# Another order of issue in the attention phase of a delta-rule attention and two gated feed-forward layers

## The chip, the cores and the metric

The kernel runs on one core of a Trainium2 chip. The metric is device time in microseconds (us), the median of several runs. The core has five engines with a queue each, worked off in order: TensorE (PE, matmuls), VectorE (DVE), ScalarE (ACT), GpSimd (POOL) and SyncE (SP, which only issues transfers here). An engine whose next instruction must wait stands still, whatever lies behind it.

## The reference

Three layers follow each other, in float32, with the weights given in float64.

```python
def _attn_ref(q, k, v, beta):                     # B, H, S, D = 4, 8, 768, 48
    k_n = k / (np.linalg.norm(k, axis=-1, keepdims=True) + 1e-06)
    state = np.zeros((B, H, D, D))
    for t in range(S):
        y[:, :, t] = einsum('bhd,bhde->bhe', q[:, :, t], state)
        v_old = einsum('bhde,bhd->bhe', state, k_n[:, :, t])
        state = state + beta_t * einsum('bhd,bhe->bhde', k_n[:, :, t], v[:, :, t] - v_old)
def _moe_ref(x, w_gate, w_val, w_out, rms_g):     # 3072 tokens, 384 -> 1536 -> 384
    xn = x / np.sqrt(np.mean(x * x, axis=-1, keepdims=True) + 1e-06) * rms_g
    g = xn @ w_gate
    return (g * sigmoid(g) * (xn @ w_val)) @ w_out
def _moe2_ref(x, w_in, w_out):                    # 384 -> 2048 -> 384
    h = x @ w_in
    return (h * tanh(softplus(h))) @ w_out
```

## The kernel before

The sequence of 768 steps is cut into 12 rows of 64 steps, for all 32 heads at once. Within a row the recurrence becomes matrix products with the inverse of a triangular 64x64 matrix per head; from row to row the state `sx` is carried. Two rows form a segment `sg`, and `rl` is a row's place in it. Everything is done in pairs of a high and a low half (`xh`, `xl`), three matmuls for one product.

The program has three phases. `phase_b1` (lines 343 to 1228) holds the attention of all rows and, beside it, the first layer's gated units of two of its six pairs of 256 columns (`part_a`, made by `gated`). `phase_b2` does the other four pairs, and `phase_c` the last layer. Weights come as 64-bit numbers and are converted on the chip, half a block at a time (`prepare_half`, `convs`): a load, a magnitude on ACT (L168; on DVE L170 where `act` is false), four bit steps on DVE (L172, L175, L180, L183), a high part on ACT (L194; or DVE) and a low part on DVE or GpSimd (L197).

The order in which instructions are issued is written by the program itself. Each strand of work is a generator that issues a piece and yields a weight. `plan` (L44) runs the strands of the start, rows 0 and 1: each has a list of times in `P`, and the strand whose next time is the lowest goes next (a time that lies before the strand's last one means: at once). `merge` (L62) runs the strands of each later row: it takes the strand with the smallest share of its total done. The numbers are arbitrary units; only the order that they give reaches the chip, and each engine works through its own part of that order.

The strands that the change and the prediction speak of:

- `quick_lane(sg)` (L761): the inverse of 16x16 blocks for rows 0 to 3, on DVE: the diagonal (ACT L626, DVE L627), transposes (L779), the scaled matrix Nw (L789 to L793), steps i2 to i7 (L802, L806), and then for each row `rl` two T8 steps (L818, L822) and two transposes (L830 to L841).
- `quick_products(r)` (L847), five calls, here a to e: a is a PE product and Zq on DVE (L863); b a product and the copy of X11 on ACT (L875); c a product, copies and the first half of `merge32` (L739); d a product and copies (L886); e the second half of `merge32` (L749, L753), after which row r's values can be computed.
- `inlane(sg)`, driven by `lanes`: the inverse for rows 4 to 11, nearly all on DVE (L627 to L719).
- `chain_row(r)`: the stages of a row, in an order given by a list of names: r residual (PE L940, DVE L945), nA and nB the norm and scaling of the keys of row r+4 (DVE L537, POOL L550, L561), q0 and q1 transposes of q (PE L620, ACT L621), y the product with the state (L958), p the scores (PE L600, DVE mask L610), v the values (PE L983, ACT L988), k the state update (PE L1032, DVE L1037), o0 and o1 the outputs (PE L999, ACT L1007, L1013), s0 and s1 their scaling (ACT L1044), x0 and x1 the input of the first layer (PE L1057, ACT L1060, then `xl`), c0 and c1 transposes of the keys of row r+4, g their products. S, T, X, Y are s0, s1, x0, x1 of the row before.
- `part_a`: gated steps of nine matmuls each (L259 to L261), with Silu on ACT (L311), and products back (L293 to L295). `DUE` says how many units of it go beside each row.

PSUM has five banks for all of the attention's products (`bank`), two for the gated units.

Of the kernel before, what the change touches and what calls it, by code (L numbers as in the profile page):

```python
# [20 lines left out]
    XB=2, WE=16, RB=4, TB=4, LANE=18.8, AFTER=6.2, LD=3.0, CVT=9.0, CVB0=0, CVB1=64.0, PSD=1, NU=4, LAG=4, XD=9, PD=12, SQ=5,  # L21
    ROW="r nA q0 q1 S p T nB y X v Y k c0 o0 c1 o1 g".split(),
    R0="r q0 q1 p v k o0 o1 s0 s1 x0 x1 c0 c1 g".split(),
    R1="r nA q0 q1 y p nB v k o0 o1 s0 s1 x0 c0 c1 g".split(),
    R2="r nA Y q0 q1 p nB y v k c0 o0 c1 o1 g".split(),
    RL="r q0 q1 S p T y X Y v o0 k o1".split(),
    DUE=[0, 6, 5, 11],
    CVS=[0, 0, 6.5, 0],
    C=dict(n=0.2, q=0.5, r=1.4, y=1.1, p=1.2, v=1.2, o=0.9, k=1.2, s=0.1, x=0.45, c=0.4, d=0.4, g=1.2, h=1.2),

    ROW0=[24.0, 24.1, 24.4, 46.4, 46.6, 48.6, 49.5, 50.0, 51.0, 51.5, 52.0, 54.0, 62.0, 62.5, 90.0],
    ROW1=[52.5, 54.5, 55.0, 55.5, 56.0, 57.0, 60.0, 60.5, 62.5, 63.5, 64.0, 65.0, 65.5, 66.0, 84.0, 84.5, 90.5],
# [66 lines left out]
def kernel(  # L99
# [17 lines left out]
    C = 64  # L117
# [225 lines left out]
    def phase_b1():  # L343
# [417 lines left out]
        def quick_lane(sg):  # L761
# [14 lines left out]
            offs = [t[:, 544:1056].rearrange("p (u c) -> p u c", c=32) for t in (N_, X_)]  # L776
            for rl in range(2):
# [31 lines left out]
            for rl in range(2):  # L809
                r = 2 * sg + rl  # L810
                Nv, Xv = Nw[:, rl], Xw[:, rl]
                for x, y, d in (
# [30 lines left out]
                )  # L843
                halves[r] = [t.rearrange("p (u c) -> p u c", c=32) for t in (Yd, YT)] + [offs[rl]]
                yield 1.75

        def quick_products(r):  # L847
# [17 lines left out]
            )  # L865
            yield 2.8
# [21 lines left out]
            yield from m32  # L888
# [9 lines left out]

# [15 lines left out]
        def chain_row(r):  # L914
# [8 lines left out]
            def turn_q(bp):  # L923
                turn(qp, bp, QT, ("Q", r, bp))
# [123 lines left out]
            def to_x(bp):  # L1048
# [12 lines left out]
                if r >= P["XD"]:  # L1061
# [48 lines left out]
        def order(r):  # L1110
            return P[f"R{r}"] if r < 3 else P["RL"] if r >= NR - 2 else P["ROW"]

# [3 lines left out]
        def finish_a(r):  # L1116
            par = tp.tile([128, KD, T], F32, tag="par", name="par", bufs=1)
# [273 lines left out]
```

## Time and profile before

| | |
|---|---|
| median of 3 runs | 1177.6 us (1176.66 to 1181.1) |
| profiled execution, its own time | 1181.6 us |
| span, first to last instruction | 1179.9 us, 33143 instructions |
| mean granted TensorE clock | 0.949 |
| PE, weight loads (PEld) | 1112.7 us (94%), 1083.1 us (92%) |
| DVE | 615.0 us (52%) |
| ACT | 387.3 us (33%) |
| POOL | 408.4 us (35%) |

The busy times are sums over the whole span, and the three phases have different limits, so the table says little about the attention phase, which takes some 440 us of it; the rows below go by stretch. A granted clock of 1.0 is 2.4 GHz, of 0.5 it is 1.2 GHz; in between is a mean over both.

### The profile page before, as it was taken

How to read it: one execution, taken by the hardware profiler on the slowest of the kernel's cores; microseconds unless marked ns; L12 is line 12 of the kernel's file. 1: busy time of each engine (PE TensorE's matmuls, PEld its weight loads, DVE VectorE, ACT ScalarE, POOL GpSimd, SP SyncE). 2: the span in 40 equal slices, each digit the busy share in tenths (PEclk: the TensorE clock that was granted, in tenths of full speed). 3: DMA queues.
4: the chain of work that ended last, by engine and by line, in shares of the span. 5: the costliest groups of instructions: out<-in, count | busy, mean ns of one | idle time of the engine just before them, and what ended most of it. 6: DMA issues, size and time to landing. Idle time of an engine off the chain costs nothing.

```text
span 1179.9 us, 33143 instructions
## 1 busy us (share of the span) xinstructions
PE 1112.7 (94%) x14712; PEld 1083.1 (92%) x14712; DVE 615.0 (52%) x1039; ACT 387.3 (33%) x822; POOL 408.4 (35%) x364
## 2 busy tenths in 40 slices
PE   5678779999999889999999999999999999999998
PEld 5677678989898889999999999999999999999998
DVE  6656798898987988777676732221111111111111
ACT  4365735676656663222222210111111111111110
POOL 2021035455432442444444432243333333333331
PEclk8656788999999999999999999999999999999999
DMA  9031323333324554443446432611110101111101
GB/s 165 3 70 42 111 56 83 83 90 80 80 83 132 155 203 159 127 142 122 130 139 204 159 122 81 228 54 41 41 41 31 27 25 41 41 41 41 41 1 27
DMA packets 130847, 104.48 MB, mean 89 GB/s; under 512 B 81008, under 2 KB 113264, under 8 KB 130704
## 3 DMA queue, kind: packets, MB, share of 16 engines
q1 hardware_dynamic: 118608, 78.77, 24.0%
q10 hardware_dynamic: 12096, 23.60, 6.1%
q8 instruction: 115, 1.88, 0.7%
q14 instruction: 28, 0.23, 0.1%
HBM read 69.31 MB, written 33.03 MB: 87 GB/s over the span
## 4 chain that ended last, share of the span: by engine, by line
PE 79%; DVE 14%; ACT 2%; SPq 2%; issue 2%; POOL 1%; DMA 0%; DVEq 0%; POOLq 0%; ACTq 0%
PE ph L260 6%; PE ph L259 6%; PE ph L261 6%; PE pd L1322 6%; PE pd L1323 6%; PE pd L1321 6%; PE pg L259 4%; PE pv L259 4%; PE pd L293 4%; PE pg L260 4%; PE pg L261 4%; PE pd L294 4%; PE pd L295 4%; PE pv L261 4%; PE pv L260 4%; DVE pr L658 2%
## 5 line engine op out<-in xcount | busy, mean ns | idle before, releaser
L1309 POOL TENSOR_TENSOR gl<-t,gh 128x512 fp32r<-128x512 f32 x96 | 123.9, 1291 | 266.0 <-DVE gh L1308 266.0
L1308 DVE CAST gh<-t 128x512 fp32r<-128x512 f32 x96 | 43.5, 456 | 328.8 <-ACT t L1303 328.8
L321 POOL TENSOR_TENSOR hl<-sg,hh 128x512 fp32r<-128x512 f32 x72 | 104.5, 1451 | 231.2 <-DVE hh L320 229.8
L1303 ACT ACTIVATE t<-ph 128x512 f32<-128x512 f32 x96 | 57.5, 599 | 346.7 <-PE ph L261 343.1
L260 PE MATMUL ph<-xl,wih 128*128 128x256 f32 x576 | 161.7, 281 | 0.0
L259 PE MATMUL ph<-xh,wih 128*128 128x256 f32 x576 | 161.6, 281 | 0.0
L261 PE MATMUL ph<-xh,wil 128*128 128x256 f32 x576 | 161.5, 280 | 0.0
L1322 PE MATMUL pd<-wql,gh 128*128 128x384 f32 x384 | 129.7, 338 | 0.0
L1323 PE MATMUL pd<-wqh,gl 128*128 128x384 f32 x384 | 129.6, 338 | 0.0
L1321 PE MATMUL pd<-wqh,gh 128*128 128x384 f32 x384 | 129.5, 337 | 0.0
L259 PE MATMUL pv<-xh,wvh 128*128 128x256 f32 x432 | 127.0, 294 | 2.2 <-DVE sg L317 2.2
L259 PE MATMUL pg<-xh,wgh 128*128 128x256 f32 x432 | 127.1, 294 | 0.0
L260 PE MATMUL pg<-xl,wgh 128*128 128x256 f32 x432 | 123.4, 286 | 1.4 <-POOL xl L1071 1.3
L261 PE MATMUL pg<-xh,wgl 128*128 128x256 f32 x432 | 123.0, 285 | 1.5 <-DVE wgl L197 1.5
L261 PE MATMUL pv<-xh,wvl 128*128 128x256 f32 x432 | 123.2, 285 | 1.2 <-DVE wvl L197 1.2
L293 PE MATMUL pd<-hh,woh 128*128 128x256 f32 x420 | 120.5, 287 | 3.0 <-DVE xl L1063 1.5
L260 PE MATMUL pv<-xl,wvh 128*128 128x256 f32 x432 | 123.0, 285 | 0.0
L311 ACT ACTIVATE sg<-pg 128x512 f32<-128x512 f32 x72 | 43.2, 601 | 236.5 <-PE pg L261 215.9
L294 PE MATMUL pd<-hl,woh 128*128 128x256 f32 x420 | 119.0, 283 | 0.0
L295 PE MATMUL pd<-hh,wol 128*128 128x256 f32 x420 | 118.7, 283 | 0.0
L261 PEld LDWEIGHTS ph<-xh,wil 128*128 128x128 f32 x576 | 108.6, 188 | 0.0
L260 PEld LDWEIGHTS ph<-xl,wih 128*128 128x128 f32 x576 | 108.4, 188 | 0.0
(208 smaller groups left out, 2617.7 us busy)
## 6 DMA issues: line engine op xcount, KB each, us to landing
raw<-in_moe_w_out_dram SPq DMA_DIRECT2D x28, 384.0 KB, 3.1
raw<-in_moe_w_in_dram SPq DMA_DIRECT2D x16, 384.0 KB, 4.5
kh<-in_k_dram SPq DMA_DIRECT2D x24, 192.0 KB, 3.9
qp<-in_q_dram SPq DMA_DIRECT2D x24, 192.0 KB, 3.6
v<-in_v_dram SPq DMA_DIRECT2D x48, 96.0 KB, 3.1
raw<-in_moe_w_gate_dram SPq DMA_DIRECT2D x12, 384.0 KB, 4.0
raw<-in_moe_w_val_dram SPq DMA_DIRECT2D x12, 384.0 KB, 3.6
xh_d<-xh SPq DMA_DIRECT2D x12, 384.0 KB, 2.4
```

The lines of the kernel that those rows point to most:

```text
L259: nc.tensor.matmul(ps[:, f, :], wh[:, kt, sl], xh[:, kt, :], start=(kt == 0), stop=False)
L260: nc.tensor.matmul(ps[:, f, :], wh[:, kt, sl], xl[:, kt, :], start=False, stop=False)
L261: nc.tensor.matmul(ps[:, f, :], wl[:, kt, sl], xh[:, kt, :], start=False, stop=(kt == KD - 1))
L293: nc.tensor.matmul(ps, wh[:, f, sl], hh[:, f, :], start=(i + f == 0), stop=False)
L294: nc.tensor.matmul(ps, wh[:, f, sl], hl[:, f, :], start=False, stop=False)
L295: nc.tensor.matmul(ps, wl[:, f, sl], hh[:, f, :], start=False, stop=last)
L321: nc.gpsimd.tensor_tensor(out=hl, in0=sg, in1=hh.bitcast(F32), op=ALU.subtract)
L1303: nc.scalar.activation(out=t, in_=ps, func=ACTF.Mish)
L1309: nc.gpsimd.tensor_tensor(out=gl, in0=t, in1=gh.bitcast(F32), op=ALU.subtract)
L1321: nc.tensor.matmul(ps, gh[:, f, sl], wh[:, f, :], start=(m + f == 0), stop=False)
L1322: nc.tensor.matmul(ps, gh[:, f, sl], wl[:, f, :], start=False, stop=False)
L1323: nc.tensor.matmul(ps, gl[:, f, sl], wh[:, f, :], start=False, stop=last and f == 1)
```

## The change

All functions stay as they are but for the numbers and lists in `P`, and for what reads them:

- Each row has its own list of stages (`R0` to `R11` in place of `R0`, `R1`, `R2`, `ROW`, `RL`), its own amount of gated units (`DUE`) and its own rate of the inverse (`LR` in place of the one `LANE`).
- The times of the start (`ROW0`, `ROW1`, `QP`, `L`, `FF`, `CV`, `K1`, `K23`, `K4`, `S`, `T`, `G`, `BL`) are new.
- The first piece of the inverse of rows 4 and 5 (`lanes`: two POOL memsets and the diagonal) is issued at the end of the start rather than in row 2.
- `xl` of rows 9, 10 and 11 is made by three ACT scalings and a POOL subtraction (L1070, L1071) rather than three DVE instructions (L1063): `XDR` is 0 for all. `PDR`: row 11's partial results are copied by DVE (L1120).
- Of the twelve weight pairs converted from row 10 on, `BAV` gives magnitude and high part of pairs 0 and 9 to DVE, and `BLV` gives the low parts of pairs 0, 5, 9 and 11 to DVE, the others to POOL (before: pairs 8 to 11 to DVE).
- Added `need(...)` and `done.add(...)` are assertions while the program is written; they issue nothing.

```diff
@@ -18,26 +18,66 @@
 
 
 P = dict(
-    XB=2, WE=16, RB=4, TB=4, LANE=18.8, AFTER=6.2, LD=3.0, CVT=9.0, CVB0=0, CVB1=64.0, PSD=1, NU=4, LAG=4, XD=9, PD=12, SQ=5,
-    ROW="r nA q0 q1 S p T nB y X v Y k c0 o0 c1 o1 g".split(),
+    LN0=0.121,
+    LNT=(102.99, 2.701),
+    FAV=[0, 0, 0, 0, 0, 0],
+    XDR=[0, 0, 0, 0, 0, 0, 0, 0, 0, 0, 0, 0],
+    PDR=[0, 0, 0, 0, 0, 0, 0, 0, 0, 0, 0, 1],
+    BLV=[1, 0, 0, 0, 0, 1, 0, 0, 0, 1, 0, 1],
+    BAV=[0, 1, 1, 1, 1, 1, 1, 1, 1, 0, 1, 1],
+    CB=[12.0, 12.0],
+    PF=[4.935, 19.846, 21.813, 15.117, 7.02],
+    XB=2,
+    WE=16,
+    RB=4,
+    TB=4,
+    LANE=18.8,
+    AFTER=6.2,
+    LD=3.605,
+    CVT=9.0,
+    CVB0=0,
+    CVB1=64.0,
+    PSD=1,
+    NU=4,
+    LAG=4,
+    SQ=5,
     R0="r q0 q1 p v k o0 o1 s0 s1 x0 x1 c0 c1 g".split(),
-    R1="r nA q0 q1 y p nB v k o0 o1 s0 s1 x0 c0 c1 g".split(),
-    R2="r nA Y q0 q1 p nB y v k c0 o0 c1 o1 g".split(),
-    RL="r q0 q1 S p T y X Y v o0 k o1".split(),
-    DUE=[0, 6, 5, 11],
-    CVS=[0, 0, 6.5, 0],
-    C=dict(n=0.2, q=0.5, r=1.4, y=1.1, p=1.2, v=1.2, o=0.9, k=1.2, s=0.1, x=0.45, c=0.4, d=0.4, g=1.2, h=1.2),
-
-    ROW0=[24.0, 24.1, 24.4, 46.4, 46.6, 48.6, 49.5, 50.0, 51.0, 51.5, 52.0, 54.0, 62.0, 62.5, 90.0],
-    ROW1=[52.5, 54.5, 55.0, 55.5, 56.0, 57.0, 60.0, 60.5, 62.5, 63.5, 64.0, 65.0, 65.5, 66.0, 84.0, 84.5, 90.5],
-    QP=[
-        [39.5, 41.0, 42.2, 43.4, 44.6], [45.3, 46.3, 47.3, 48.3, 49.3],
-        [66.0, 68.0, 70.0, 71.5, 73.0], [73.2, 75.0, 76.5, 78.0, 79.5],
-    ],
-    L=[(20.0, 1.08), (46.5, 1.15)], FF=(80.5, 3.2),
-    CV=[21.0, 22.0, 23.0, 73.2, 74.8, 76.4, 77.8, 77.9, 78.0] + [79.5 + 0.9 * i for i in range(40)],
-    K1=[7.3, 9.95, 10.0, 10.6], K23=[11.95, 13.2, 15.1, 16.0], K4=[30.0, 47.0, 50.2, 53.0], S=[0, 11.0, 22.0, 23.0, 54.0],
-    T=[9.9, 13.0, 25.5, 26.0], G=[12.0, 15.0, 27.5, 28.0], BL=29.0, CVN=12.9,
+    R1="r nA q0 q1 y v p nB o0 o1 s0 s1 k x0 c0 c1 g".split(),
+    R2="nA r Y q0 q1 p nB y v k c0 o1 c1 g o0".split(),
+    R3="r q0 q1 S nA p T nB y X v Y k c0 o0 c1 o1 g".split(),
+    R4="nA r q0 q1 S T p nB y X v Y k c0 o0 c1 o1 g".split(),
+    R5="r nA q0 q1 p S T nB y v X Y c0 o0 k o1 c1 g".split(),
+    R6="nA r q0 q1 S T p y X v nB Y k c0 o0 c1 o1 g".split(),
+    R7="r nA q0 q1 S p nB T v y X o0 Y c0 c1 k o1 g".split(),
+    R8="r nA q0 S q1 T p y nB X v Y c1 o0 k o1 g c0".split(),
+    R9="q0 nA q1 r S nB p T y X Y v k c0 o0 c1 g o1".split(),
+    R10="q0 q1 r S p T X v Y y o0 k o1".split(),
+    R11="S r q0 q1 p T y X Y v o0 k o1".split(),
+    DUE=[-2.078, 6, 4.883, 10.883, 10.883, 10.883, 10.883, 10.279, 8.191, 10.779, 10.947, 11.898],
+    CVS=[-0.772, 23.215, 8.774, -10.747, -1.817, -3.119, -5.758, -18.924, -8.547, -7.362, -6.242, 0],
+    LR=[0.954, 27.435, 20.59, 16.189, 19.235, 14.5, 18.8, 16.357, 36.841, 19.4, 46.383, 52.328],
+    C={'n': 0.17, 'q': 0.5, 'r': 1.4, 'y': 1.1, 'p': 1.2, 'v': 1.2, 'o': 0.9, 'k': 1.2, 's': 0.172, 'x': 0.45, 'c':
+        0.4, 'd': 0.238, 'g': 1.2, 'h': 1.754},
+    ROW0=[22.93, 15.452, 28.121, 44.741, 47.548, 48.766, 45.738, 33.435, 53.633, 48.929, 54.116, 57.767, 62.484,
+        37.473, 85.635],
+    ROW1=[53.942, 53.85, 45.563, 56.778, 52.975, 35.612, 56.216, 58.146, 61.312, 39.939, 40.485, 58.417, 58.232,
+        63.245, 75.692, 84.258, 88.776],
+    QP=[[37.444, 41.0, 43.125, 21.565, 37.63], [45.22, 48.268, 45.506, 51.903, 54.368], [66.04, 61.517, 70.739,
+        71.533, 71.42], [71.511, 74, 75, 77.393, 79.5]],
+    L=[(20.85, 1.08), (45.092, 1.188)],
+    FF=(81.208, 4.33),
+    CV=[21.0, 16.511, 23.0, 73.2, 74.618, 57.385, 77.618, 77.869, 83.198, 79.553, 80.453, 82.487, 82.253, 83.153,
+        84.053, 84.953, 83.189, 83.862, 87.653, 87.329, 89.491, 90.258, 91.253, 75.729, 75.875, 77.529, 78.019,
+        69.055, 80.493, 75.943, 90.497, 102.298, 101.376, 98.806, 107.967, 63.817, 97.364, 105.683, 106.789,
+        100.504, 100.996, 101.937, 102.837, 90.131, 105.198, 102.676, 132.795, 107.284, 104.921],
+    K1=[2.295, 9.567, 8.05, 2.905],
+    K23=[11.95, 14.08, 13.659, 16.0],
+    K4=[32.11, 47.0, 50.2, 39.074],
+    S=[0, 11.0, 24.718, 22.326, 51.748],
+    T=[9.259, 12.574, 26.491, 31.494],
+    G=[12.0, 15.225, 21.198, 32.131],
+    BL=35.919,
+    CVN=12.955,
 )
 
...
             yield 2.0
-            yield from m32
+            next(m32)
+            done.add(("hq", r))
+            yield 1.5
+            for _ in m32:
+                pass
...
-                if r >= P["XD"]:
+                if P["XDR"][r]:
...
         def order(r):
-            return P[f"R{r}"] if r < 3 else P["RL"] if r >= NR - 2 else P["ROW"]
+            return P[f"R{r}"]
...
-                (nc.vector.tensor_copy if r >= P["PD"] else nc.scalar.copy)(par[:, o, :], ps)
+                (nc.vector.tensor_copy if P["PDR"][r] else nc.scalar.copy)(par[:, o, :], ps)
...
+        lane, laned, left = lanes(iter(())), [0.0], []
             (budget(part_a, P["DUE"][1]), P["FF"]),
+            (until(lane, laned, P["LN0"]), P["LNT"]),
         )
-        lane, laned, left = lanes(iter(())), [0.0], []
...
-                    streams.append((until(lane, laned, upto), P["LANE"]))
+                    streams.append((until(lane, laned, upto), P["LR"][r]))
                 elif rl == 0:
                     st_i.close()
-                    streams.append((seq(left.pop(), delay(7.0)), 13.0))
+                    streams.append((seq(left.pop(), delay(P["PF"][4])), P["PF"][3]))
                     wbp.append(st_b.enter_context(pool("wbA")))
                     todo = [(c, m, cols(w, m)) for m in range(FA, NP1) for c, w in (("g", w_gate), ("v", w_val))]
                     todo += [("o", m, rows(w_out1, m)) for m in range(FA, NP1)]
                     gens = []
                     for i, (c, m, cut) in enumerate(todo):
-                        if 2 * i < WE:
-                            gens.append(prepare(lambda: wbp[0], (c, m), cut, tag="wb", bufs=WE))
-                        else:
-                            gens.append(prepare(lambda: wbp[1], (c, m), cut, low=nc.vector, tag="wb", bufs=2 * len(todo) - WE))
+                        x, n = (0, WE) if 2 * i < WE else (1, 2 * len(todo) - WE)
+                        gens.append(prepare(
+                            lambda x=x: wbp[x], (c, m), cut, act=bool(P["BAV"][i]),
+                            low=nc.vector if P["BLV"][i] else None, tag="wb", bufs=n,
+                        ))
                     cv = convs(gens)
-                    streams.append((budget(cv, 0.75 * WE), 0.75 * WE))
+                    streams.append((budget(cv, P["CB"][rl]), P["CB"][rl]))
                 else:
-                    streams.append((budget(cv, 0.75 * WE), 0.75 * WE))
+                    streams.append((budget(cv, P["CB"][rl]), P["CB"][rl]))
                 merge(*streams)
         last = [x for x in LATE.values() if x in late]
         run(*[late[x]() for x in last if x[0] == "s"])
...
-        run(budget(part_a, 3))
+        run(budget(part_a, P["PF"][0]))
...
-        merge((part_a, 19.0), (seq(budget(cv, P["CVT"]), delay(1)), P["CVT"] + 1))
+        merge((part_a, P["PF"][1]), (seq(budget(cv, P["CVT"]), delay(P["PF"][2])), P["CVT"] + 1))
```

## Rows read from the trace of the kernel before

**Rows 1.** Busy us by stretch, granted clock (PEclk), DMA share, GB/s
```profile
core 0: us, PE busy (x) PEld busy (x) DVE busy (x) ACT busy (x) POOL busy (x), PEclk, DMA share, GB/s
113.00:140.00 27.00, 22.74 (x579) 21.52 (x579) 20.50 (x41) 17.97 (x33) 2.91 (x3) 0.71 0.34 105
140.00:200.00 60.00, 46.23 (x915) 42.38 (x919) 58.83 (x88) 27.62 (x68) 23.66 (x16) 0.83 0.34 81
200.00:360.00 160.00, 158.04 (x3895) 146.38 (x3888) 140.42 (x188) 107.84 (x250) 72.54 (x59) 1.00 0.31 79
360.00:460.00 100.00, 89.55 (x1451) 83.69 (x1450) 85.69 (x152) 59.15 (x139) 37.62 (x38) 0.97 0.50 162
460.00:1180.00 720.00, 715.42 (x5460) 715.09 (x5458) 237.83 (x423) 117.68 (x212) 251.25 (x212) 1.00 0.26 83
```

**Rows 2.** Timeline of DVE: start us, us, instruction, [idle before <-releaser]
```profile
41.69 1.04 DVE L841 STREAM_TRANSPOSE A<-e 128x512 f32<-128x512 f32 x1
...
58.77 0.69 DVE L863 TENSOR_TENSOR Zq<-pp,qc 128x512 f32<-128x512 f32 x1 [8.76 <-PE pp L858]
...
63.86 1.28 DVE L627 SCALAR_TENSOR_TENSOR compq<-A,h,compq 128x1024 f32<-128x1024 f32 x1 [3.21 <-ACT compq L626]
...
71.16 0.48 DVE L789 TENSOR_SCALAR N__178<-dq,qc 128x512 f32<-128x512 f32 x1
...
79.64 1.02 DVE L945 TENSOR_TENSOR v<-v,pp 128x384 f32<-128x384 f32 x2 [6.48 <-PE pp L940]
...
88.94 1.02 DVE L818 TENSOR_TENSOR prq<-N__178,X__179 128x512 f32<-128x512 f32 x1
...
104.19 1.04 DVE L841 STREAM_TRANSPOSE A<-e 128x512 f32<-128x512 f32 x1
...
112.91 0.69 DVE L863 TENSOR_TENSOR Zq<-pp,qc 128x512 f32<-128x512 f32 x1 [7.69 <-PE pp L858]
```

**Rows 3.** Timeline of ACT, 55 to 63, three rows one behind the other
```profile
55.39 1.18 ACT L753 COPY A<-pp 32x512 f32<-32x512 f32 x2 [0.68 <-PE pp L749]
61.48 1.18 ACT L875 COPY X11q<-pp 32x512 f32<-32x512 f32 x2 [4.91 <-PE pp L858]
62.68 1.15 ACT L626 ACTIVATE compq<-A,h 128x1024 f32<-128x1024 f32 x1
```

**Rows 4.** Timeline of PE, 46 to 124, starts and lengths of groups
```profile
46.83 1.76 PE L858 MATMUL pp<-Zq,A 32*32 32x32 f32 x58 [3.65 <-DVE Zq L863]
...
58.28 0.43 PE L858 MATMUL pp<-A,X__179 32*32 32x32 f32 x15 [1.54 <-issue]
...
59.51 1.92 PE L858 MATMUL pp<-Zq,A 32*32 32x32 f32 x64 [0.80 <-DVE Zq L863]
...
66.48 1.74 PE L858 MATMUL pp<-A,Zq 32*32 32x32 f32 x58
...
68.15 1.96 PE L1032 MATMUL pp<-ve,kh 64*64 64x48 f32 x64
...
71.88 3.22 PE L999 MATMUL pp<-ve,PT 128*64 128x96 f32 x32
...
123.48 0.58 PE L259 MATMUL pg<-xh,wgh 128*128 128x256 f32 x1
```

**Rows 5.** Lines 1063, 1071, 197: ns min/median/max, first and last start us
```profile
L1063 DVE SCALAR_TENSOR_TENSOR xl<-pp,gT,xh x18: 341/341/351, 389.1 to 434.4; 128x128 fp32r<-128x128 f32 x18
...
L1071 POOL TENSOR_TENSOR xl<-xf,xh x18: 993/1340/2077, 79.5 to 359.9; 128x384 fp32r<-128x384 f32 x18
...
L197 DVE TENSOR_TENSOR wol<-t,woh x12: 495/552/1824, 149.2 to 468.7; 128x384 fp32r<-128x384 f32 x12
```

**Rows 6.** Timeline of PE: a step's first of nine matmuls, what follows them
```profile
128.80 0.37 PE L259 MATMUL pv<-xh,wvh 128*128 128x256 f32 x1
...
130.04 1.16 PE L600 MATMUL pp<-kT 64*64 64x64 f32 x64
```

**Rows 7.** Two neighbours among windows of 5 us, columns as in the first group
```profile
155.00:160.00 5.00, 1.53 (x67) 1.24 (x65) 4.79 (x12) 0.00 (x0) 1.19 (x1) 0.93 0.91 200
160.00:165.00 5.00, 3.24 (x67) 2.94 (x68) 4.90 (x9) 2.31 (x5) 1.98 (x2) 0.50 0.14 27
```

More of the change, by code (lines that the diff above doesn't have):

```diff
@@ L585, in products @@
             need(("T", r, 0), ("T", r, 1))
+            if sg == 2:
+                need(("hq", rl), ("hq", 2 + rl))
             gram(("G", r), kT_t[r], kT_t[r], None, A_t[sg][:, rl * 16:rl * 16 + 16, :], swap=True)
@@ L776, in quick_lane @@
             offs = [t[:, 544:1056].rearrange("p (u c) -> p u c", c=32) for t in (N_, X_)]
+            if sg:
+                need(("off", 0), ("off", 1))
             for rl in range(2):
@@ L811, in quick_lane @@
                 Nv, Xv = Nw[:, rl], Xw[:, rl]
+                if sg:
+                    need(("hq", rl))
                 for x, y, d in (
@@ L843, in quick_lane @@
                 )
+                done.add(("ql", r))
                 halves[r] = [t.rearrange("p (u c) -> p u c", c=32) for t in (Yd, YT)] + [offs[rl]]
@@ L865, in quick_products @@
             )
+            done.add(("off", r))
             yield 2.8
@@ L897, in lanes @@
         def lanes(ending):
+            need(("off", 2), ("off", 3), ("ql", 3))
             nc.gpsimd.memset(X_, 0.0)
@@ L923, in turn_q @@
             def turn_q(bp):
+                if bp:
+                    need(("Q", r, 0))
                 turn(qp, bp, QT, ("Q", r, bp))
@@ L994, in outputs @@
                 need(("v", r), ("p", r), ("y", r) if r else ("p", r))
+                if r == 0 and bp:
+                    need(("o", r, 0))
                 if r == 0 and bp == 0:
@@ L1116, in finish_a @@
         def finish_a(r):
+            need(("hq", 2), ("hq", 3))
             par = tp.tile([128, KD, T], F32, tag="par", name="par", bufs=1)
             def finish(o, ps):
-                (nc.vector.tensor_copy if r >= P["PD"] else nc.scalar.copy)(par[:, o, :], ps)
+                (nc.vector.tensor_copy if P["PDR"][r] else nc.scalar.copy)(par[:, o, :], ps)
                 if o == KD - 1:
@@ L1135, in phase_b1 @@
         for m in range(FA):
-            gens.append(prepare(lambda: wa, ("g", m), cols(w_gate, m), low=nc.vector))
-            gens.append(prepare(lambda: wa, ("v", m), cols(w_val, m), low=nc.vector))
+            gens.append(prepare(lambda: wa, ("g", m), cols(w_gate, m), act=not P["FAV"][2 * m], low=nc.vector))
+            gens.append(prepare(lambda: wa, ("v", m), cols(w_val, m), act=not P["FAV"][2 * m + 1], low=nc.vector))
         for m in range(FA):
-            gens.append(prepare(lambda: wa, ("o", m), rows(w_out1, m), low=nc.vector))
+            gens.append(prepare(lambda: wa, ("o", m), rows(w_out1, m), act=not P["FAV"][4 + m], low=nc.vector))
         cv = convs(gens, 3)
```

## The prediction

> **What bounds the kernel now.** I read the span by stage first, then the stage with most to win engine by engine, then who waits for whom there. From 460 us to the end TensorE (PE) is busy 715.42 of 720 us at full clock, and between 200 and 360 us 158.04 of 160 [rows 1]. Nothing that the change touches can shorten those stretches by more than their 2 us of holes; but they also pass on one for one whatever is won ahead of them. What can be won lies in two places. Until 200 us PE is partly idle and mostly at a low granted clock, and VectorE (DVE) sets the end: from 140 to 200 us it is busy 58.83 of 60 us [rows 1]. From 360 to 460 us PE is idle 10.45 us, at a clock of 0.97 [rows 1].
>
> So the question for the first place is when DVE gets to the full stretch, and that the reader sees in its idle time before it [rows 2]: it stands still for 8.76 us before the second quick product's Zq, 3.21 us before the second quick inverse's diagonal, 6.48 us before row 1's residual and 7.69 us before the last Zq, together 26.1 us. In each it waits for something that was ready to be issued in another place. The clearest is the second: ScalarE's (ACT's) copy that starts the diagonal needs nothing but the key products of rows 2 and 3, yet stands in ACT's queue behind the copy of X11 at 61.48, which waited 4.91 us for PE [rows 3].
>
> **The change, part by part.** No function gains or loses an instruction: the added `need` and `done` are assertions of the program that writes the kernel. The order of issue follows from the yields and the numbers. Many new numbers change no order: negative conversion shares, the rates of the inverse in rows 0, 1, 10 and 11, and the delay of 21.8 after the last conversions, all set nothing. The rest falls into three terms.
>
> *Term 1, start-up (all that comes before 140 us).* Step by step:
> 1. Call a of quick_products(0) moves ahead of the rest of quick_lane(0)'s row 1. Its Zq (0.69 us, as the next one's) can follow the transpose with which row 0 ends, at 42.73 [rows 2]: done at 43.5. PE's next group, which started at 46.83 after 3.65 us of waiting for that Zq [rows 4], starts 3.3 us sooner, and PE then works without a break to the end of row 0's quick products. The row 1 steps of DVE now come behind Zq and lose as much, but they had an idle 8.76 us behind them. Gain: 3.3 us.
> 2. The diagonal of quick_lane(1) is issued ahead of quick_products(1). ACT can do it right after its copy at 55.39 (1.18 us long), which itself comes 3.3 us sooner: 55.39 + 1.18 - 3.3 = 53.3 instead of 62.68 [rows 3]. DVE's part moves from 63.86 to about 54.5 [rows 2], 9.4 us.
> 3. That does not all survive, because the next step (Nw, 71.16 [rows 2]) stands behind row 0's state update on DVE, as before. On PE, row 0's values now go ahead of call b, and the state update and outputs 0 and 1 ahead of call d, so PE's chain up to the update loses d only. Call a of quick_products(1) ends at 58.71 - 3.3 = 55.4; b, the values and c with its merge take 66.48 - 59.51 = 6.97 us in either order, the update 1.96 [rows 4]: 64.4. Nw follows its end at 70.11 by 1.05 us, so now at 65.4, 5.7 us sooner.
> 4. Row 1's residual now comes after step i5 of quick_lane(1), not before i2, so the 6.48 us of waiting at 79.64 [rows 2] go: PE finishes outputs (3.22 us), d (66.48 to 68.15, 1.67 us) and the residual's matmuls (of one kind with the update, 1.96 us) [rows 4] at 71.3, and DVE comes to them later. What holds DVE instead is the root of row 4's norm, which stands on ACT behind the outputs' copies: outputs end at 67.6, and I allow 2 us for these, 69.6. From the residual's end to the first T8 step DVE had 88.94 - 80.66 = 8.3 us of work [rows 2], which is still all to be done: 77.9 instead of 88.94, 11 us.
> 5. Now PE is late. Row 1's values are issued ahead of its scores, so that the values no longer wait for DVE's mask, but by the same adding up the scores are ready only at about 80.5, and the state update of row 1, now behind outputs 0 and 1, at 87.2. Before each, DVE waits some 1.8 us (my estimates). The 16.3 us from the first T8 step to the last transpose (88.94 to 105.23) [rows 2] become 19.9: it ends at 97.8, 7.4 us sooner.
> 6. Call a of quick_products(3) goes ahead of d and e of quick_products(2), so the last Zq comes at about 101 instead of 112.91 [rows 2], but d and e are then still to be done: PE's first gated step moves from 123.48 [rows 4] to about 115.
>
> So PE is 8 us sooner and DVE's conversions 12 us; as DVE sets the end from here on, I take 10 us. The lower bound is step 1 alone, 3.3; the upper one has nearly all of the 26.1 us gone, 22. From 113 to 140 us DVE has 6.5 us of holes [rows 1]. The gated steps are issued further apart there (4.33 against 3.2 units), so that ACT's Silu stands less often before a conversion; the first diagonal of the inverse of rows 4 and 5 moves to the end of this stretch. DVE's work is the same. I take nothing, between -4 and +4.
>
> *Term 2, 140 to 360 us.* The stages of rows 2 to 9 change places by one to three positions each, and the inverse is issued somewhat later in rows 3 and 5 and much sooner in row 8. In 140 to 200 us DVE has only 1.2 us to lose, in 200 to 360 us PE has 2 us [rows 1], so a better order can give 3 us at most; a worse one costs a few us where a stage is put too close behind what it needs (in row 6 the scaling of the next keys stands only two stages before their transpose). I take nothing, with 3 on either side.
>
> *Term 3, 360 to 460 us.* The low halves of x for rows 9 to 11 leave DVE: 18 instructions of 0.341 us, 6.1 us, become 18 scalings on ACT (59.15 us busy of 100 [rows 1]) and six subtractions on GpSimd of 0.99 to 2.08 us [rows 5]. They are needed a row later, so ACT and GpSimd hide them; if not, the last costs up to 2.1 us. Against that, magnitude and high part of one weight pair come to DVE in row 10 and of one in the tail, bounded by 0.495 and 1.824 us for each of the four instructions of a pair [rows 5]; at the median of 0.552, 2.2 us. The low parts of two pairs come to DVE and those of two others leave it in the tail. DVE is left with about 2 us less in rows 10 and 11. Two gated steps move out of row 8, where PE is full, to rows 9 to 11, where it has holes; one of nine matmuls takes about 1.24 us [rows 6], so 2.5 us. These overlap; I take 3 us, between +4 and -10 (nearly all the idle time).
>
> Sum: -10 + 0 - 3 = -13 us. The profiled execution took 1181.6 us, so 1168.6; the median of the runs is 4.0 below that execution, which gives 1164.6.
>
> **The rivals.**
> *More of it: 0.12.* PE's scores and update of row 1 come as early as DVE's steps, so the whole of step 4 and 5 is kept and the DVE waits of [rows 2] shrink by 22 us. For it: in step 5 I laid every PE group end to end at the low clock, and an earlier rise shortens them. Against it: PE's own work there. 1177.6 - 22 - 3 = 1152.6.
>
> *Little of it: 0.18.* DVE and PE only exchange who waits: after step 1 the next wait takes its place at once, for row 1's scores and update, since two PSUM banks of the state's product are held until the outputs and the scores have to wait for ACT to empty those of the values. Then only the 3.3 us of step 1 remain: 1177.6 - 3.3 = 1174.3, within half a per cent.
>
> *The clock: 0.08, and slower.* PE falls to its lower level of 1.2 GHz after a pause (1.53 us busy of 5 at 155 us, then a granted clock of 0.50 [rows 7]). In the new order the gated steps, PE's only dense work before 140 us, come in smaller portions between waits for conversions. If the clock stayed low from 113 to 200 us, PE's 22.74 us at 0.71 and 46.23 at 0.83 [rows 1] would be 32.3 + 76.7 = 109 us in a stretch of 87: PE would be the bound, 22 us later. With the 13 us won: +9, 1186.6. It decides when the low clock holds for more than 13 of these 22 us. Against it: rows 2 and 3 issue the same gated steps as before.
> The Trainium skill (TensorE: Matmul & The Clock Gate, section "What's actually happening") says that the throttled state is the default and that activity releases it; the trace agrees with its 0.50 after a nearly idle stretch, and the rule speaks for this rival.
>
> *The shared port: 0.06.* A subtraction of x on GpSimd takes 0.993 us at best and 2.077 at worst [rows 5]. If it holds up DVE just as it is held up, six of them cost DVE up to 6 x 1.08 = 6.5 us while it is on the path in rows 10 and 11: 1164.6 + 6.5 = 1171.1.
> The Trainium skill (SBUF — State Buffer, section "SBUF: two separate sides") calls the port pair that VectorE and GpSimd share an exclusive lock; the spread agrees with it, but no row here shows DVE being the loser at this place.
>
> **How the numbers follow.** The forecast case has 0.56, and its own range is 1158 to 1170. About 0.5% (5.9 us) is what a measurement tells from no change, so faster means below 1171.7: forecast, more, half of the port and a little of the small case, 0.73; slower is the clock, 0.08; 0.19 remain. The range reaches from the larger gain to the small one, 1150 to 1177, and leaves out the clock and the tail of the larger gain.
>
> **What would show it.** Right: the diagonal of quick_lane(1) on ACT near 53 us, the wait of 6.48 us before row 1's residual gone, the last Zq near 101 us, PE's first gated step near 115, DVE full from about 130 to 190 us, and the first window with PE full starting near 190. Wrong: a first gated step still near 120 us (little of it), a granted clock of 0.5 beyond 140 us (the clock), or PE holes after 360 us larger than 10 us.

## The result: 16 us faster, and the profile after

The changed kernel takes 1163.3 us (median of four runs, 1162.5 to 1163.7), the kernel before 1179.4 in the same comparison (1176.7 to 1181.4): a ratio of 0.9864, with an interval of 0.9839 to 0.9889. That is 16.1 us, where the prediction had 13 and a time of 1164.6; from the 1177.6 that it started from, it is 14.3. The profiled execution has a span of 1160.8 us, at a mean granted clock of 0.959. In the changed kernel's source most of the functions stand 40 to 56 lines lower: Zq is L910 now, the diagonal L668 and L669, Nw L833, the residual L999, the state update L1093, the scores' mask L652, a low part L237.

The stretches of [rows 1] in the changed kernel, busy us by stretch, and the granted clock as the third figure from the end:

```profile
core 0: us, PE busy (x) PEld busy (x) DVE busy (x) ACT busy (x) POOL busy (x), PEclk, DMA share, GB/s
113.00:140.00 27.00, 19.51 (x400) 17.64 (x394) 22.32 (x43) 19.51 (x39) 7.62 (x6) 0.82 0.28 90
140.00:200.00 60.00, 53.18 (x1221) 48.89 (x1223) 56.51 (x81) 33.87 (x74) 24.06 (x20) 0.92 0.34 75
200.00:360.00 160.00, 154.54 (x3750) 142.27 (x3751) 144.52 (x196) 103.49 (x246) 70.94 (x57) 1.00 0.35 93
360.00:460.00 100.00, 95.30 (x1399) 91.16 (x1394) 91.44 (x151) 56.41 (x144) 46.45 (x42) 1.00 0.53 170
460.00:1160.00 700.00, 696.31 (x5300) 695.98 (x5299) 223.72 (x402) 111.29 (x200) 245.24 (x208) 1.00 0.25 81
```

From 140 to 200 us PE does 53.18 us of work at a clock of 0.92 where it did 46.23 at 0.83; from 360 to 460 us it has 4.7 us of holes where it had 10.45 [rows 1]. These are the two places that the prediction named. (The second pair is not the same work: the attention phase ends some 18 us sooner in these two profiles. From the end of the seventh group of copies into `par` to that of the last, PE is idle 5.2 us of 96 now and was idle 10.6 us of 107.) From 200 to 360 us it has lost a little: 5.5 us idle in place of 2.

How the start came forward is seen in DVE's rows (start, length, instruction, idle time before it), which answer to [rows 2]:

```profile
40.73 0.68 DVE L910 TENSOR_TENSOR Zq<-pp,qc 128x512 f32<-128x512 f32 x1
...
53.30 1.28 DVE L669 SCALAR_TENSOR_TENSOR compq<-A,h,compq 128x1024 f32<-128x1024 f32 x1 [3.83 <-ACT compq L668]
...
64.97 1.02 DVE L1093 TENSOR_TENSOR sx<-sx,pp 128x384 f32<-128x384 f32 x2 [6.68 <-PE pp L1088]
65.90 0.48 DVE L833 TENSOR_SCALAR N__178<-dq,qc 128x512 f32<-128x512 f32 x1
...
73.41 1.02 DVE L999 TENSOR_TENSOR v<-v,pp 128x384 f32<-128x384 f32 x2
...
82.01 1.29 DVE L652 TENSOR_TENSOR PT<-pp,mpos 128x512 f32<-128x512 f32 x2 [3.38 <-PE pp L642]
...
88.24 1.02 DVE L1093 TENSOR_TENSOR sx<-sx,pp 128x384 f32<-128x384 f32 x2 [0.98 <-PE pp L1088]
...
97.61 1.04 DVE L887 STREAM_TRANSPOSE A<-e 128x512 f32<-128x512 f32 x1
101.68 0.69 DVE L910 TENSOR_TENSOR Zq<-pp,qc 128x512 f32<-128x512 f32 x1 [3.04 <-PE pp L905]
...
115.68 1.03 DVE L237 TENSOR_TENSOR wgl<-t,wgh 128x384 fp32r<-128x384 f32 x2 [7.76 <-ACT wgh L234]
```

Of the four large waits of [rows 2] three are gone or smaller: 8.76 us before the second Zq to 0.30, 6.48 before row 1's residual to nothing, 7.69 before the last Zq to 3.04; the diagonal's stays (3.21, now 3.83), some 10.6 us earlier. Others have grown: 6.68 us before row 0's state update (2.35 before) and 3.38 before row 1's scores. All of DVE's waits for other engines from 40 to 125 us together fell only from 32.7 to 28.3 us, so most of the waiting has moved and not gone. The last row is new to the prediction: DVE has its bit steps of the first weights done at 107.9 us and then stands still for 7.76 us, because ACT's high part comes late. ACT's rows tell why, and PE's show the first gated step:

```profile
52.12 1.15 ACT L668 ACTIVATE compq<-A,h 128x1024 f32<-128x1024 f32 x1
...
112.17 0.58 ACT L663 COPY kT<-pp 128x512 f32<-128x512 f32 x1
113.95 1.16 ACT L934 COPY A<-pp 32x512 f32<-32x512 f32 x2 [1.20 <-PE pp L905]
115.14 0.93 ACT L234 CAST wgh<-t 128x384 fp32r<-128x384 f32 x2
```

```profile
115.70 0.58 PE L299 MATMUL pg<-xh,wgh 128*128 128x256 f32 x1 [0.26 <-ACT wgh L234]
```

The cast of the high part needs nothing but DVE's bit steps, yet it stands in ACT's queue behind the copies of the quick products of rows 2 and 3, most of which wait for PE. It is the pattern of [rows 3] once more, at another place.

### The profile page after: what moved, and what is told of

The parts are those of the page before. It is cut to its first block, busy times and chain, and to the rows that moved or that the text cites. A ratio compares the mean times of both kernels' runs of the same rounds, so it can differ in the third digit from the quotient of the medians.

```text
span 1160.8 us, 33146 instructions
## 1 busy us (share of the span) xinstructions
PE 1104.4 (95%) x14712; PEld 1073.8 (93%) x14712; DVE 616.4 (53%) x1032; ACT 385.8 (33%) x829; POOL 414.5 (36%) x370
## 4 chain that ended last, share of the span: by engine, by line
PE 78%; DVE 12%; ACT 4%; issue 2%; POOL 1%; DMA 1%; SPq 1%; POOLq 0%; DVEq 0%; ACTq 0%
PE ph L300 6%; PE ph L299 6%; PE ph L301 6%; PE pd L1381 6%; PE pd L1382 6%; PE pd L1380 6%; PE pv L299 4%; PE pd L333 4%; PE pg L299 4%; PE pg L300 4%; PE pv L300 4%; PE pv L301 4%; PE pd L334 4%; PE pg L301 4%; PE pd L335 4%; DVE pr L700 2%
## 5 line engine op out<-in xcount | busy, mean ns | idle before, releaser
L1367 DVE CAST gh<-t 128x512 fp32r<-128x512 f32 x96 | 43.5, 456 | 328.8 <-ACT t L1362 328.8
```

## The experiments

All of them are the changed kernel's program with numbers and lists of `P` exchanged for those of the kernel before, or new ones. Their lines are numbered 7 lower than the changed kernel's. Each ratio is against runs of the kernel before on the same chip in the same session (medians 1178.9, 1177.9 and 1179.4 in the three sessions).

**The start alone.** The kernel before with all the new times of the start, and R1; rows 2 to 11 and the engines as before.

```diff
-    R1="r nA q0 q1 y p nB v k o0 o1 s0 s1 x0 c0 c1 g".split(),
+    R1="r nA q0 q1 y v p nB o0 o1 s0 s1 k x0 c0 c1 g".split(),
...
-    L=[(20.0, 1.08), (46.5, 1.15)], FF=(80.5, 3.2),
+    L=[(20.85, 1.08), (45.092, 1.188)],
+    FF=(81.208, 4.33),
```

> The kernel before with the new start alone (the times and the list of rows 0 and 1 and the early first piece of the inverse; rows 2 to 11 and the engines as before). Start-up theory (the forecast's): the start carries nearly all, 10 us of the 16, and the median is 9 to 14 us under the kernel before. Shared theory: the changed kernel's products back of the first layer end 8 us sooner for row 0 and 17 us sooner for row 11, so the later lists bring as much; this one gains only 6 to 9 us. Little-of-it: at most 4 us. In the trace the first gated step should start near 115 us, as in the changed kernel.

Measured: 1167.1 us, 0.9895 (0.9879 to 0.991), 11.8 us faster (10.6 to 14.3 by its interval). The start carries most of the change, and its first gated step is at 114.72 us.

**Rows alone, engines alone, both without the start.** The lists R2 to R11 with DUE, LR, CVS and the costs; then XDR, PDR, BLV, BAV and PF; then both together.

```diff
-    R2="r nA Y q0 q1 p nB y v k c0 o0 c1 o1 g".split(),
+    R2="nA r Y q0 q1 p nB y v k c0 o1 c1 g o0".split(),
...
```

```diff
-    XDR=[0, 0, 0, 0, 0, 0, 0, 0, 0, 1, 1, 1],
+    XDR=[0, 0, 0, 0, 0, 0, 0, 0, 0, 0, 0, 0],
...
```

> The kernel before with the lists of stages, amounts of gated units and rates of the inverse of rows 2 to 11 alone (start and engines as before). Start-up theory: no more than 3 us either way, since VectorE and TensorE have no more than 3 us to give from 140 to 360 us. Shared theory: 4 to 8 us faster.

> The kernel before with the moves between engines alone (low halves of x of rows 9 to 11 to ScalarE and GpSimd, row 11's copies to VectorE, four weight pairs, and the tail's numbers). Start-up theory: 1 to 3 us faster, from some 2 us less of VectorE work in rows 10 and 11. Shared theory: 3 to 6 us faster. Shared-port theory: up to 4 us slower, with subtractions of x on GpSimd near 2 us and VectorE's two-input instructions beside them longer than their median.

> The changed kernel with the start of the kernel before. Start-up theory: it loses 9 to 14 us, that is 2 to 6 us under the kernel before. Shared theory: it loses 6 to 9 us and stays 7 to 10 us under the kernel before. If the parts only work together, it is as slow as the kernel before.

Measured: rows alone 1174.8, 0.9968 (0.9955 to 0.9981); engines alone 1179.2, 1.0003 (0.9991 to 1.0015); both 1168.6, 0.9915 (0.9901 to 0.9929). The start-up theory missed on the last two: the engines alone bring nothing where it had 1 to 3 us, and rows and engines bring 10 us without the new start, where it had 2 to 6; that is the shared theory's range, and more than twice the sum of the two alone. And with the start alone the parts add up to 22 us, where the change brings 16: some of the gain can be had in two ways, but only once.

**One step of the start, then three.** Call a of `quick_products(0)` alone (step 1 of the prediction); then with it the diagonal (step 2) and row 1's residual (step 4).

```diff
-        [39.5, 41.0, 42.2, 43.4, 44.6], [45.3, 46.3, 47.3, 48.3, 49.3],
+        [37.444, 41.0, 42.2, 43.4, 44.6], [45.3, 46.3, 47.3, 48.3, 49.3],
```

```diff
-    ROW1=[52.5, 54.5, 55.0, ...
+    ROW1=[53.4, 54.5, 55.0, ...
...
-    L=[(20.0, 1.08), (46.5, 1.15)], FF=(80.5, 3.2),
+    L=[(20.0, 1.08), (45.0, 1.15)], FF=(80.5, 3.2),
```

> The kernel before with step 1 alone (the first time of the first quick product 37.444 in place of 39.5, so that its Zq goes ahead of row 1's T8 steps on VectorE). Start-up theory: 3.3 us sooner at TensorE's first matmul behind that Zq, and as the four waits behind it are untouched, 1 to 3 us in the median. Little-of-it theory: this is where the start's whole gain comes from, 8 us or more. Third: VectorE loses as much as TensorE wins, no change.

> The kernel before with steps 1, 2 and 4 (also the second quick inverse 1.5 units sooner, so that its diagonal goes ahead of the second quick product, and row 1's residual at 53.4, behind i5): ScalarE's diagonal near 53 us, the 6.48 us of waiting before the residual shorter. Start-up theory: these three waits are two thirds of it, 5 to 9 us faster. Exchange theory: without the new order of row 1's own stages the next wait takes their place and it gains no more than step 1 alone.

Measured: 1176.1, 0.9984 (0.9974 to 0.9994), and 1174.9, 0.9966 (0.9954 to 0.9979): by the ratios 1.9 us and 4.0 us (0.7 to 3.1 and 2.5 to 5.4 by the intervals; the medians differ by 1.8 and 3.0). The second is less than the start-up theory's 5 to 9 and more than step 1 alone. DVE's rows of the second kernel show where the rest went:

```profile
55.61 1.28 DVE L662 SCALAR_TENSOR_TENSOR compq<-A,h,compq 128x1024 f32<-128x1024 f32 x1 [4.55 <-ACT compq L661]
68.26 1.02 DVE L1086 TENSOR_TENSOR sx<-sx,pp 128x384 f32<-128x384 f32 x2 [6.86 <-PE pp L1081]
...
77.68 1.02 DVE L992 TENSOR_TENSOR v<-v,pp 128x384 f32<-128x384 f32 x2 [1.56 <-PE pp L987]
...
108.65 0.69 DVE L903 TENSOR_TENSOR Zq<-pp,qc 128x512 f32<-128x512 f32 x1 [8.63 <-PE pp L898]
```

The diagonal comes 8.2 us sooner than in [rows 2], but row 0's state update then costs DVE 6.86 us (2.35 before), and at the last Zq it waits 8.63 us where it waited 7.69: that Zq is 4.3 us sooner and no more. Against the three experiments with the old start, where the diagonal is at 61.88 to 62.53 us and the last Zq at 110.50 to 111.23, it is 6 to 7 us and 2 to 3 us. The next wait takes the place of the one removed as long as PE's groups stay where they are.

**The middle rows as before.** The changed kernel with R2 to R7, CVS and the first eight LR as before.

```diff
-    R2="nA r Y q0 q1 p nB y v k c0 o1 c1 g o0".split(),
+    R2="r nA Y q0 q1 p nB y v k c0 o0 c1 o1 g".split(),
...
```

> The changed kernel with the lists of stages, the rates of the inverse and the conversion share of rows 2 to 7 as before. Theory: with the new start these lists bring nothing, since VectorE or TensorE is full there, so it is as fast as the changed kernel, within 1.5 us. Rival: they bring the 4 us that the lists of rows 2 and 3 brought with the old start, and it is 3 to 5 us slower than the changed kernel.

Measured: 1162.0, 0.9861 (0.9844 to 0.9879), the changed kernel's ratio. With the new start the new order of rows 2 to 7 brings nothing. With the old one all the new rows brought 4.1 us. The two are not the same set, since rows 8 to 11 and the amounts of gated units stay new here; but the end of the first-layer products beside row 1 (the second of the groups of copies into `par`) is at 206.2 us in the kernel with the rows alone, and at 209.5 in the one with the engines alone, which starts in the same way: in these two profiles 3.3 us are won by 206 us, in the stretch that the new start improves too.

**The low halves of x back on DVE.** The changed kernel with this alone undone.

```diff
-    XDR=[0, 0, 0, 0, 0, 0, 0, 0, 0, 0, 0, 0],
+    XDR=[0, 0, 0, 0, 0, 0, 0, 0, 0, 1, 1, 1],
```

> The changed kernel with the low halves of x of rows 9 to 11 on VectorE again, 18 instructions of 0.34 us. Theory: VectorE's queue is on the path in rows 9 to 11, so 3 to 6 us slower than the changed kernel (that is what the moves between engines brought with the new lists). Rival: the weight pairs that change engine made that gain, and this is within 1.5 us of the changed kernel.

Measured: 1168.4, 0.9915 (0.9901 to 0.9929). Without this one move the changed kernel loses 6 of its 16 us, and is no better than the start alone. Two windows of it, and the same two of the changed kernel behind them:

```profile
380.00:400.00 20.00, 17.58 (x321) 16.47 (x314) 19.45 (x33) 10.14 (x24) 11.32 (x12) 0.91 0.48 152
400.00:420.00 20.00, 17.48 (x199) 16.19 (x198) 17.37 (x34) 12.98 (x34) 6.40 (x9) 0.91 0.49 163
```

```profile
380.00:400.00 20.00, 19.45 (x385) 18.20 (x384) 19.45 (x33) 13.96 (x38) 12.54 (x12) 1.00 0.48 142
400.00:420.00 20.00, 17.52 (x159) 16.44 (x159) 17.13 (x29) 14.00 (x41) 10.88 (x12) 1.00 0.57 198
```

DVE is as busy in both (19.45 us in the first window), so what it does for x it does in place of other work. PE has 1.9 us more of holes in the first window, and the granted clock is 0.91 in both windows instead of 1.00, so that even in the second one 17.48 busy us hold less work. The ends of the groups of copies into `par` say where the loss lies: the eighth ends at 374.7 us here and at 374.6 in the changed kernel, the last at 447.7 and 441.1. So all of it comes behind the eighth, where x of rows 9 to 11 is made.

**The start with the engines.** The start alone, and XDR, PDR, BLV, BAV and PF as in the change; rows 2 to 11 as before. The edit is that of the engines alone, on the kernel with the new start.

> The new start and the moves between engines, with the old lists of rows 2 to 11. Theory: the low halves of x on ScalarE pay only with the new lists of rows 8 to 11 (alone they gave nothing), so it is within 2 us of the new start alone, 10 to 13 us under the kernel before. Rival: it was the old start that hid their gain, and this one is as fast as the changed kernel, 15 to 17 us under the kernel before.

Measured: 1171.4, 0.992 (0.9902 to 0.9939), some 3 us slower than the start alone; the intervals (to 0.991 there, from 0.9902 here) overlap a little. That is neither what the theory had (within 2 us of the start alone) nor the rival (as fast as the changed kernel): in the old order the engines' moves cost, if anything. In the profiles the two kernels are level up to the ninth group of copies into `par` (400.6 and 400.7 us), and 3.0 us apart at the tenth (424.9, 421.9). From 400 to 430 us PE is busy 25.68 us here, at a clock of 0.87 in the last ten, and 28.17 in the start alone, at 1.00. Which wait begins the loss, the runs do not settle. One wait that the start alone does not have is DVE's for ACT's Silu, 5 us behind row 11's outputs. DVE's row and then ACT's:

```profile
429.64 0.69 DVE L350 TENSOR_TENSOR sg<-sg,pv 128x512 f32<-128x512 f32 x1 [5.01 <-ACT sg L344]
```

```profile
422.38 0.37 ACT L1170 COPY par<-pd 128x256 f32<-128x256 f32 x1 [3.02 <-PE pd L328]
424.53 0.37 ACT L1170 COPY par<-pd 128x256 f32<-128x256 f32 x1 [1.78 <-PE pd L328]
425.92 0.89 ACT L1109 ACTIVATE xh<-pp,gT 128x128 fp32r<-128x128 f32 x3 [1.01 <-PE pp L1106]
426.68 0.89 ACT L1119 ACTIVATE xf<-pp,gT 128x128 f32<-128x128 f32 x3
...
428.18 0.95 ACT L1119 ACTIVATE xf<-pp,gT 128x128 f32<-128x128 f32 x3
428.93 0.68 ACT L344 ACTIVATE sg<-pg 128x512 f32<-128x512 f32 x1
```

ACT's copies wait for PE, and then the new scalings `xf`, twice 0.75 us, stand ahead of the Silu that DVE waits for. It is not shown to be the cause: PE itself waits only 0.28 us for that Silu, and the kernel with the engines alone has the same 5.0 us and loses nothing.

**Conversions and gated steps of the start as before.** The start alone without CV, FF and CVN.

```diff
-    FF=(81.208, 4.33),
+    FF=(80.5, 3.2),
...
```

> The new start alone, but with the old times of the conversions and of the gated steps. Theory: the start's gain is the order of the quick inverse, the quick products and the stages of rows 0 and 1, so it keeps at least 9 of the 11.8 us. Rival: the wider spacing of gated steps and the order of the conversions after 113 us make a good part, and it keeps 7 us or less.

Measured: 1171.4, 0.993 (0.9913 to 0.9947): 8.1 us faster than before, not 11.8. The order of conversions and gated steps is worth some 4 us, between what the theories expected; the next kernel, run beside this one with the new conversions, measured 1167.0, 4.3 us less.

**The last calls as before.** The start alone without the new times of `quick_products(2)` and `(3)` (step 6).

```diff
-    [66.04, 61.517, 70.739, 71.533, 71.42], [71.511, 74, 75, 77.393, 79.5]],
+    [66.0, 68.0, 70.0, 71.5, 73.0], [73.2, 75.0, 76.5, 78.0, 79.5]],
```

> The new start alone, but with the old times of the quick products of rows 2 and 3 (step 6 undone: call a of the last one behind d and e of the one before). Theory: the last Zq comes some 5 us later, TensorE's first gated step about 1 to 3 us later, since d and e have to be done either way; 1 to 4 us slower than the new start. Rival: VectorE's lead at the last Zq is lost anyway while it waits for ScalarE's high parts (8 to 9 us), so no more than 1 us slower.

Measured: 1167.0, 0.9897 (0.9881 to 0.9913), the same as with it, as the rival had it; a difference below some 2.5 us would not show. DVE's waits from 40 to 125 us, in total, times and the longest, of the start alone and then of this kernel:

```profile
DVE wgl L230 <- ACT wgh L227: 9.0, 1, 9.0
...
DVE Zq L903 <- PE pp L898: 3.4, 1, 3.4
```

```profile
DVE Zq L903 <- PE pp L898: 7.3, 1, 7.3
...
DVE wgl L230 <- ACT wgh L227: 2.6, 1, 2.6
DVE wvl L230 <- ACT wvh L227: 2.6, 1, 2.6
```

3.9 us less before the last Zq are 6.4 us more before the first low part. With step 6 the last Zq starts 6.2 us sooner (99.42, 105.57 without), the first low part does not (114.70, 114.45): what step 6 wins for DVE is lost in the next wait.

**The first casts on DVE.** Magnitude and high part of the first two weight pairs on DVE, right behind the last Zq, in the kernel with the middle rows as before.

```diff
-    FAV=[0, 0, 0, 0, 0, 0],
+    FAV=[1, 1, 0, 0, 0, 0],
...
-    CV=[21.0, 16.511, 23.0, 73.2, ...
+    CV=[72.9, 72.9, 72.9, 73.2, ...
```

> A new version: the changed kernel with the old lists of rows 2 to 7, and with magnitude and high part of the first two weight pairs on VectorE, issued behind the last Zq, where it waits 7.8 to 8.5 us for ScalarE's high parts. Theory: VectorE is the bound from there to 190 us, so it is sooner by these 8 us less eight more instructions of about 0.4 us: 3 to 5 us faster than the changed kernel, 19 to 21 us under the kernel before. Rival: TensorE's end of the quick products sets the first gated step anyway, and VectorE's lead is lost in the next wait: within 1.5 us of the changed kernel.

Measured: 1160.9 (1158.7 to 1163.2), 0.984 (0.9819 to 0.9861). It is the lowest time here, but its interval overlaps those of the changed kernel and of the one that it is built on, so a gain of 2 or 3 us is not resolved. DVE's wait for the high part is 0.8 us there in place of 8.5 (7.8 in the changed kernel), and its first low part is at 109.92 us in place of 114.83. But a wait of 3.0 us for a magnitude on ACT has come up, PE's first gated step is no sooner (115.97 us; 114.85 before the edit, 115.70 in the changed kernel), and the last group of copies into `par` ends at 441.0 us, 440.6 before the edit.

## Why the prediction was right

**Term 1, the start: forecast 10 us, measured 11.8 alone.** In the changed kernel's profile the steps lie within 1.5 us of the forecast: the diagonal on ACT at 52.1 us (53.3), Nw at 65.9 (65.4), the residual without a wait and the first T8 step at 76.9 (77.9), the scores' mask at 82.0 (80.5, with 3.38 us of waiting instead of 1.8), row 1's state update at 88.2 (87.2), the last transpose's end at 98.7 (97.8), the last Zq at 101.7 (101) and the first gated step at 115.7 (115). So the mechanism was right, but a closeness of 1 us is luck. The five kernels with this start (the changed one, the start alone, the middle rows as before, the low halves of x back, the start with the engines) have the last Zq between 99.42 and 102.81 us and the first gated step between 113.89 and 117.56. And two errors cancel: the first Zq is done at 41.4 us, 2.1 us ahead of the forecast 43.5, and Nw follows it by 24.5 us, not by 21.9, so that steps 2 and 3 were taken 2.6 us too short. For the last Zq and the first gated step the prediction shows no sum.

"PE is 8 us sooner and DVE's conversions 12 us" did not come, and the 10 us in between were taken without a working. In the four profiles with the old start (before, rows alone, engines alone, both) the first gated step is at 120.79 to 123.48 us and the first low part at 118.13 to 120.54; the means of the five with the new one are 6.2 us and 3.6 us sooner. For DVE this is because ACT's casts stood behind waiting copies; step 6, which was to make the 7.4 us of step 5 into 12, is worth nothing by itself that the runs resolve.

The rest of the gain comes later. Set against the engines alone, the start alone is 7.0 us ahead at the end of the first group of copies into `par` (171.1, 178.1) and 9.4 us at the third (228.8, 238.2), and stays so up to the seventh. This is the second error of the forecast, of the other sign: the order of the conversions and gated steps, "I take nothing, between -4 and +4", is worth some 4 us (8.1 instead of 11.8 without it). Without it the first two groups end at 172.6 and 203.9 us, with it at 171.1 and 201.2, and the spans of the two profiles differ by the same 2.7 us (1168.4, 1165.7). By which instruction, the runs do not settle.

Step 1 was also priced too high as a lower bound: 3.3 us forecast, 1.9 measured (0.7 to 3.1 by its interval).

**The sum.** It adds the terms as if they were independent, and they are not: on top of the new rows and engines the new start is worth 6 us (0.9915 to 0.9864), not 11.8. That what is won ahead is passed on one for one holds, from the second group of copies into `par` on: these two kernels are 6.1 us apart there and 5.7 us at the last (446.8, 441.1). The overlap lies ahead of it, where the new start and the new rows each win some of the same time. That the forecast of the whole came out is the work of terms 1 and 3, each within 2 us.

**Term 2, 140 to 360 us: forecast nothing, measured nothing** beside the new start, for the orders of rows 2 to 7.

**Term 3, from row 8 on: forecast 3 us, measured 3.7** (0.9864 against 0.9895 for the start alone), give or take 3.5 by the two intervals; in the profiles the last group of copies into `par` ends at 441.1 us, 444.6 in the start alone. Its working was too simple. It took the engines' moves as a saving of DVE time and the gated steps' new places as another; alone the moves bring nothing or cost up to 3 us, and the new lists with all moves but that of `xl` cost some 2 (0.9915 against 0.9895; the intervals overlap). Only together do they win. The move of `xl` is worth 6 us in the new order; that this is because ACT and GpSimd have room where it is put is a reading that no run shows. The new start with the new lists and no move at all was not run, nor the amounts of gated units or the weight pairs by themselves.

**The rivals.** *Little of it* is true of any one step: three of them bring 4 us. It fails for the whole, since the change moves PE's groups as well. *More of it* would have needed PE to keep up with DVE; PE did not, with 6.68 us before row 0's update and 3.38 before the scores. *The clock* did not come as a loss of time, though what it rests on did, and its sign (the low level again behind 140 us) in part. Windows of ten us of the changed kernel:

```profile
110.00:120.00 10.00, 9.74 (x189) 9.12 (x184) 3.10 (x7) 8.02 (x16) 0.00 (x0) 0.53 0.07 23
120.00:130.00 10.00, 9.19 (x235) 8.01 (x233) 9.39 (x22) 8.87 (x16) 0.00 (x0) 1.00 0.51 160
130.00:140.00 10.00, 3.59 (x51) 3.11 (x49) 9.83 (x16) 4.95 (x13) 7.62 (x6) 0.82 0.23 81
140.00:150.00 10.00, 6.12 (x159) 5.65 (x163) 9.59 (x26) 2.02 (x4) 0.00 (x0) 0.67 0.32 81
150.00:160.00 10.00, 8.40 (x140) 7.47 (x130) 9.83 (x15) 4.24 (x10) 4.54 (x4) 0.83 0.46 80
160.00:170.00 10.00, 9.21 (x251) 8.63 (x249) 9.90 (x12) 5.14 (x13) 3.36 (x4) 1.00 0.11 23
```

The clock rises from 0.53 to 1.00 with the first gated steps, falls to 0.67 behind a stretch with 3.59 busy us of 10, and stays at 1.00 from 160 us on, with PE busy 9.2 us or more of 10 in the windows up to 220. Before, the same windows still had 0.70 from 160, 0.83 from 180 and 0.83 from 190 us, and stayed at 1.00 from 200 to 360. The other signs came too: DVE is busy 9.59 us or more of each ten from 130 to 190 us, and the first window with PE busy for all of its 10 us is that from 190. The Trainium skill (TensorE: Matmul & The Clock Gate, section "What's actually happening") has the throttled state as the default that activity releases; the 0.67 behind the nearly idle window agrees, but the 0.53 of a window with 9.74 busy us does not follow from it. The fall comes behind a wait that the prediction did not have. PE, and then ACT, around 138 us:

```profile
137.98 1.46 PE L642 MATMUL pp<-QT,kT 64*64 64x64 f32 x32 [5.85 <-ACT QT L663]
```

```profile
134.88 0.51 ACT L234 CAST woh<-t 128x384 fp32r<-128x384 f32 x1 [2.98 <-DVE t L223]
...
137.30 0.62 ACT L663 COPY QT<-pp 128x512 f32<-128x512 f32 x1
140.56 0.51 ACT L234 CAST woh<-t 128x384 fp32r<-128x384 f32 x1 [2.63 <-DVE t L223]
140.98 0.58 ACT L663 COPY QT<-pp 128x512 f32<-128x512 f32 x1
```

Row 2's copies of q stand behind casts that wait for DVE, and PE loses 5.85 and 2.17 us. DVE is full meanwhile (9.83 of 10 us), so I take it that this costs little now; no run takes the wait away.

*The shared port* did not make the change slower than forecast, but what it rests on is there. The six subtractions took 1014 to 1253 ns, near the best of [rows 5]; it is DVE that is held up. Beside five of the six a bit step of DVE takes 0.48 to 0.82 us longer than the same instruction elsewhere, 3.4 us together, over half of the 6.1 us that DVE saves:

```profile
L1127 POOL TENSOR_TENSOR xl<-xf,xh x6: 1014/1140/1253, 372.1 to 419.5; 128x384 fp32r<-128x384 f32 x6
```

```profile
372.46 1.07 DVE L212 TENSOR_SCALAR t<-t 128x384 f32<-128x384 f32 x1
...
377.36 1.26 DVE L223 SCALAR_TENSOR_TENSOR t<-raw,t 128x384 int32<-128x384 int32 x1
...
397.47 0.35 DVE L212 TENSOR_SCALAR t<-t 128x384 f32<-128x384 f32 x1
397.85 1.05 DVE L215 TENSOR_SCALAR t<-t 128x384 int32<-128x384 int32 x1
```

GpSimd subtracts from 372.06 to 373.31, from 377.11 to 378.21 and from 397.51 to 398.69 us. Undisturbed, L212 takes 0.35 us as at 397.47, L215 0.36 and L223 0.56. The prediction put none of this into its sum; the 6 us of the move are what is left with it.

## What to carry to other kernels

In an in-order queue, look for the instruction that could go but stands behind one that waits; move it, and at once work out what waits next, since one move alone mostly exchanges one wait for another. Price a reordering from the chain of the engine that is then late, group by group; that gave each step of the start to 1.5 us in one profile and to 3 us over five. A move of work between engines and a new order can each be worth nothing or a loss alone and some 4 us together, so parts are tried alone, together and taken away one at a time, and their gains are not added.

## What the runs showed of the hardware that was not expected

The start differs between executions of the same instructions: PE's first gated step is at 123.48 us in the profile of the kernel before [rows 4], but at 120.80, 120.97 and 120.79 in three experiments whose start is the same, and from 113.89 to 117.56 in the five with the new start. A difference of 2 or 3 us at one place between two profiles is therefore no finding by itself; the gains in total time above are from medians of several runs.

DVE instructions beside GpSimd work took up to three times as long (L212 1.07 us at 372.46, 0.35 at 397.47). From 345 to 441 us of the changed kernel 26 of them take over 0.1 us more than the shortest of their kind, 19.4 us in all, and each of the 26 overlaps a GpSimd instruction on tensors; in the kernel before, from 352 to 460 us, there are 20 such, with 15.4 us. Low parts on GpSimd stand beside them as well as subtractions of x, so work moved to GpSimd was not free for DVE here.
